# Loading the third batch's q between the W1 chunks of the second batch, and moving beta's split to GpSimd

## Chip, cores, metric

One Trainium2 chip (trn2), one core. The metric is the device time of one execution in microseconds. Executions of one kernel agree within about 0.3%, so differences of 2 us (0.25%) are read here from several rounds against the kernel before on the same chip, and from the traces. Faster or slower is drawn at 2%, or 16 us.

## The reference

Grouped-query attention, then a residual MLP with affine scalings, for 8 batches of 384 rows.

```python
# q [8,16,384,64], k and v [8,4,384,64] float32
scores = matmul(q, k^T) / 8            # k, v repeated 4 times over the heads
x = softmax(scores) @ v                # -> [8, 384, 1024]
a1 = alpha1 * x + beta1
u = x + lam * einsum('ts,bsd->btd', w_tok, a1)
a2 = alpha2 * u + beta2
out = u + lam * (relu(a2 @ w_ch1) @ w_ch2)   # w_ch1 [1024,4096], w_ch2 [4096,1024]
```

## The kernel before

Each batch has two passes on TensorE (PE). In the first, the **W1 pass**, `a2 @ w_ch1` is done in 16 chunks of W1, each 16 matmuls, 2.60 us. W1 does not stay in SBUF: every batch streams it again from HBM, through a ring of five chunk tiles, cast from float32 to bf16 on the way. In the second, the **W2 pass**, PE multiplies by `w_ch2` (which stays in SBUF), and between its matmuls stand the scores, exponentials and token mixing of the next batch. The first batch's attention has no pass to hide in; that is the **lead**.

q and k must stand transposed. From the third batch on, a DMA transpose (a **flip**) does that, from a raw bf16 copy; for the first two batches PE does it.

```python
def load_q(b):                       # four loads of 192 KB, issued by GpSimd
    qrs[b] = sb.tile([P, Hq, NST, D], bf, tag="q_raw", name="q_raw", bufs=1)
    for h in range(0, Hq, G):
        nc.gpsimd.dma_start(out=qrs[b][:, h:h + G], in_=q[b, h:h + G]...)

def flip_queue(b):
    return nc.scalar if b == 2 else nc.sync

# main(b), W1 pass
for c in range(NCH):                 # NCH = 16 chunks, RING = 5
    ...                              # 16 matmuls, evictions on ScalarE and VectorE in turn
    if b or c + RING < NCH:
        load_w1(b * NCH + c + RING)  # into the tile that chunk c has just freed
    if b == 0 and c == NCH - 1:
        for i in range(RING):
            load_w1(NCH + i)
        load_next(2)                 # place k, load q and v of the third batch
# ... the flips of the third batch, placed at steps of the second batch's W1 pass
if b == 1:
    moves = [(0, 46 + 4 * i, flip_q, 2, 2 * i - 2, 2) if i else (0, 46, flip_k, 2) for i in range(5)]

# lead: rows of alpha, beta, lambda are split into bf16 parts on VectorE
def split(lo, hi, step=None):
    ...
    nc.vector.tensor_copy(out=rows_b[:32, c], in_=src[:, c])
    nc.vector.scalar_tensor_tensor(out=dst[:, c], in0=rows_b[:32, c], scalar=m, in1=src[:, c], op0=MUL, op1=subtract)
```

The softmax here doesn't subtract the row's maximum and nothing guards it: scores larger than these inputs give would overflow.

## Time and profile before

| | |
|---|---|
| median (9 runs beside each later set) | 806.1 to 806.6 us |
| span of the profiled run | 803.5 us |
| PE busy | 793.8 us |
| first W1 matmul of the main loop (the lead's end) | 38.48 us |
| first matmul of the second batch's W1 pass | 133.44 us |
| first scores matmul of the third batch | 178.42 us |
| from the one to the other ("the stretch") | 44.98 us |
| the same stretch one batch later | 42.56 us |

"The stretch" holds one W1 pass, four matmuls of the W2 pass and any wait for the third batch's q. Everything else of the second batch cancels out of it. The profile lines are in the prediction. To read the timeline lines: start, length, engine, source line, operation, output<-inputs, shape, count, and in brackets how long the engine was idle before and what ended that.

### The profile page before, as it was taken

How to read it: one execution, taken by the hardware profiler on the slowest of the kernel's cores; microseconds unless marked ns; L12 is line 12 of the kernel's file. 1: busy time of each engine (PE TensorE's matmuls, PEld its weight loads, DVE VectorE, ACT ScalarE, POOL GpSimd, SP SyncE). 2: the span in 40 equal slices, each digit the busy share in tenths (PEclk: the TensorE clock that was granted, in tenths of full speed). 3: DMA queues.
4: the chain of work that ended last, by engine and by line, in shares of the span. 5: the costliest groups of instructions: out<-in, count | busy, mean ns of one | idle time of the engine just before them, and what ended most of it. 6: DMA issues, size and time to landing. Idle time of an engine off the chain costs nothing.

```text
span 803.5 us, 14220 instructions
## 1 busy us (share of the span) xinstructions
PE 793.8 (99%) x6123; PEld 452.0 (56%) x6123; DVE 343.5 (43%) x669; ACT 226.9 (28%) x309; POOL 178.5 (22%) x233
## 2 busy tenths in 40 slices
PE   8999999999999999999999999999999999999997
PEld 4766555655556555565555655566555655556545
DVE  8652465215552266322662236622366225552122
ACT  6624431223402233123221233122431223312100
POOL 7234231332013500135002340033400330003000
PEclk9999999999999999999999999999999999999999
DMA  9999999999269972999439991499914995129611
GB/s 190 202 186 202 205 207 170 187 186 170 66 126 188 198 101 58 162 189 196 74 73 169 193 196 43 92 174 197 163 46 114 165 198 88 48 61 187 82 40 40
DMA packets 234975, 113.17 MB, mean 141 GB/s; under 512 B 84376, under 2 KB 228768, under 8 KB 234912
## 3 DMA queue, kind: packets, MB, share of 16 engines
q0 software_dynamic: 170752, 83.47, 79.1%
q1 hardware_dynamic: 58848, 27.22, 13.5%
q10 hardware_dynamic: 5312, 1.57, 1.5%
q8 instruction: 48, 0.79, 0.4%
q14 instruction: 15, 0.12, 0.0%
HBM read 170.53 MB, written 12.58 MB: 228 GB/s over the span
## 4 chain that ended last, share of the span: by engine, by line
PE 84%; DMA 10%; issue 3%; DVE 1%; POOL 1%; ACT 0%; POOLq 0%
PE ch L443 37%; PE h L410 34%; DMA w<-in_moe_w_ch_dram 8%; PE sc L217 4%; PE sc L252 3%; PE sc L273 3%; DMA qT<-q_raw 1%; POOL w L136 1%; PE h L168 1%; PE tok L273 1%; PE av L252 0%; PE warm L460 0%; PE ut L290 0%; PE tp L203 0%; ACT hT L226 0%
## 5 line engine op out<-in xcount | busy, mean ns | idle before, releaser
L443 PE MATMUL ch<-w,hT 128*128 128x512 bf16 (+2 forms) x1600 | 357.7, 371 | 1.1 <-DVE o L448 0.9
L410 PE MATMUL h<-a2T,w 128*128 128x384 bf16 (+1 forms) x2016 | 331.5, 326 | 0.8 <-ACT hT L418 0.8
L410 PEld LDWEIGHTS <-w 128*128 128x128 bf16 x2016 | 196.8, 98 | 131.2 <-issue 1.5
L443 PEld LDWEIGHTS <-hT 128*128 128x128 bf16 x1600 | 144.6, 98 | 153.1 <-issue 10.5
L136 POOL DMA_DIRECT2D w<-in_moe_w_ch_dram x128 | 112.1, 878 | 519.3 <-PE h L410 500.5
L226 ACT ACTIVATE es<-sc 128x1024 bf16<-128x1024 f32 x126 | 121.4, 1023 | 187.9 <-PE sc L217 175.8
L420 DVE TENSOR_SCALAR hT<-h,bias 128x384 bf16<-128x384 f32 x128 | 79.1, 618 | 218.3 <-PE h L410 217.7
L418 ACT ACTIVATE hT<-h,bias 128x384 bf16<-128x384 f32 x128 | 74.3, 580 | 304.9 <-PE h L410 299.4
L448 DVE TENSOR_TENSOR o<-ch,vecs 128x512 f32<-128x512 f32 (+2 forms) x50 | 33.4, 669 | 107.8 <-PE ch L443 107.8
L252 PEld LDWEIGHTS <-es 128*128 128x128 bf16 x1008 | 38.2, 97 | 13.2
L273 PEld LDWEIGHTS <-wtokT 128*128 128x128 bf16 x576 | 37.3, 98 | 13.8 <-DVE x L258 1.7
L217 PE MATMUL sc<-qT,kT 64*128 64x384 bf16 (+2 forms) x576 | 41.9, 272 | 0.7 <-DMA qT<-q_raw 0.6
L257 DVE RECIPROCAL rinv<-sc 128x6 f32<-128x6 f32 x56 | 10.8, 193 | 68.4 <-PE sc L252 67.5
L252 PE MATMUL sc<-v,es 128*128 128x65 bf16 x1008 | 39.9, 193 | 0.0
L280 DVE TENSOR_TENSOR x<-sc,x 128x384 f32<-128x384 f32 x56 | 31.0, 553 | 20.0 <-PE sc L273 20.0
L273 PE MATMUL sc<-a,wtokT 128*128 128x128 bf16 x504 | 37.3, 219 | 0.0
L217 PEld LDWEIGHTS <-kT 64*128 64x128 bf16 x576 | 21.6, 94 | 24.5 <-issue 18.2
L449 DVE TENSOR_TENSOR o<-o,x 128x512 f32<-128x512 f32 (+2 forms) x50 | 33.5, 670 | 1.7
L284 DVE TENSOR_TENSOR a<-x,vecs 128x384 bf16<-128x384 f32 x56 | 32.7, 584 | 1.9
L265 DVE TENSOR_TENSOR a1f<-x,vecs 128x384 f32<-128x384 f32 x56 | 31.2, 558 | 1.9
L267 DVE TENSOR_TENSOR a<-a1f,vecs 128x384 bf16<-128x384 f32 x56 | 31.2, 558 | 1.9
L258 DVE TENSOR_TENSOR x<-sc,rinv 128x384 f32<-128x384 f32 x56 | 31.2, 558 | 1.9
(75 smaller groups left out, 203.1 us busy)
## 6 DMA issues: line engine op xcount, KB each, us to landing
w<-in_moe_w_ch_dram POOLq DMA_DIRECT2D x144, 512.0 KB, 8.6
out_dram<-o SPq DMA_DIRECT2D x47, 256.0 KB, 2.0
q_raw<-in_q_dram POOLq DMA_DIRECT2D x28, 192.0 KB, 8.1
kst<-in_k_dram SPq DMA_DIRECT2D x16, 192.0 KB, 3.4
v<-in_v_dram POOLq DMA_DIRECT2D x24, 64.0 KB, 7.9
a2T<-a SPq DMA_TRANSPOSE x56, 2.3
qg<-in_q_dram POOLq DMA_DIRECT2D x3, 192.0 KB, 5.9
stage<-in_q_dram ACTq DMA_DIRECT2D x2, 192.0 KB, 3.7
```

The costliest lines, as they stand in the source:

```text
L136: nc.gpsimd.dma_start(out=t, in_=w1src[:, :, c * CW * P:(c + 1) * CW * P])
L217: nc.tensor.matmul(out=sc[:, hh, k % 4:k % 4 + n], lhsT=kT[r, sk, 2 * p // G, :], rhs=qT[r, p, st:st + n, :], start=True, stop=True)
L226: nc.scalar.activation(out=e, in_=sc, func=EXP, scale=scale_qk)
L252: nc.tensor.matmul(out=av[:, hh, sq, :], lhsT=ess[k // 4][:, m % 2, k % 4, :], rhs=vb[:, sk, hk, :], start=(sk == 0), stop=(sk == NST - 1))
L273: nc.tensor.matmul(out=ps[:, tt, :], lhsT=wtokT[:, st, tt * P:(tt + 1) * P], rhs=a1s[p][:, st, :], start=(st == 0), stop=(st == NST - 1 an ...
L284: nc.vector.tensor_tensor(out=a2s[p], in0=u, in1=bc(al2, p), op=MUL)
L410: nc.tensor.matmul(out=ps[:, :n], lhsT=w1[:, dt, j * P:(j + 1) * P], rhs=a2T[:, dt, :n], start=(dt == 0), stop=(dt == NDT - 1))
L418: nc.scalar.activation(out=hT[:, nt, :], in_=ps[:, :S], func=RELU, bias=c1)
L420: nc.vector.tensor_scalar(out=hT[:, nt, :], in0=ps[:, :S], scalar1=c1, scalar2=0.0, op0=ADD, op1=mybir.AluOpType.max)
L443: nc.tensor.matmul(out=ps[:, lo:hi], lhsT=hT[:, nt, ms * P:(ms + 1) * P], rhs=w2[:, nt, dw * 512 + lo:dw * 512 + hi], start=(nt == 0), sto ...
L448: nc.vector.tensor_tensor(out=o[:, lo:hi], in0=ps[:, lo:hi], in1=lam_t[:, c], op=MUL)
L449: nc.vector.tensor_tensor(out=o[:, lo:hi], in0=o[:, lo:hi], in1=x[:, ms, c], op=ADD)
```

## The change

Its intent: take the flips of the third batch off ScalarE's queue, where each holds up evictions for 3 us; load q later, in small parts, out of the way of the W2 loads; and relieve VectorE in the lead.

```diff
-    def load_q(b):
-        qrs[b] = sb.tile([P, Hq, NST, D], bf, tag="q_raw", name="q_raw", bufs=1)
-        for h in range(0, Hq, G):
+    def load_q(b, hs=range(0, Hq, G)):
+        if b not in qrs:
+            qrs[b] = sb.tile([P, Hq, NST, D], bf, tag="q_raw", name="q_raw", bufs=1)
+        for h in hs:
...
-        flip_queue(b).dma_start_transpose(...)      # flip_k and flip_q
+        nc.sync.dma_start_transpose(...)
...
                     load_w1(NCH + i)
-                load_next(2)
+                place_k(2, 0)
+                place_k(2, 1)
+                load_v(2)
+            if b == 1 and c in (3, 5, 7, 9):
+                load_q(2, [(c - 3) * 2])
...
-                moves = [(0, 46 + 4 * i, flip_q, 2, 2 * i - 2, 2) if i else (0, 46, flip_k, 2) for i in range(5)]
+                moves = [(0, 1, flip_k, 2)] + [(0, 46, flip_q, 2, i, 2) for i in range(0, NP, 2)]
... lead: beta's rows on GpSimd, W1 chunks 2 to 4 asked for after them
-        for c in range(RING):
+        load_w1(0)
+        load_w1(1)
+        place_k(0, 1)
+        scale_rows(1, nc.gpsimd)
+        split(1, 2, None, nc.gpsimd)
+        for c in range(2, RING):
             load_w1(c)
-        place_k(0, 1)
... lead: the order of scores, a1, token mixing (18 steps; cut); a part of q asked for before w_tok (cut);
... on GpSimd the split uses two instructions for each scalar_tensor_tensor (cut)
```

More of the change, by code (lines that the diff above doesn't have):

```diff
@@ L41 @@
     ADD = mybir.AluOpType.add
+    SUB = mybir.AluOpType.subtract
     B, Hq, S, D = q.shape
@@ L110, in load_v @@
             nc.gpsimd.dma_start(out=vt[b % 2][:, st, :, :D], in_=by_st(v[b])[:, st])
-    def load_q(b):
-        qrs[b] = sb.tile([P, Hq, NST, D], bf, tag="q_raw", name="q_raw", bufs=1)
-        for h in range(0, Hq, G):
+    def load_q(b, hs=range(0, Hq, G)):
+        if b not in qrs:
+            qrs[b] = sb.tile([P, Hq, NST, D], bf, tag="q_raw", name="q_raw", bufs=1)
+        for h in hs:
             nc.gpsimd.dma_start(out=qrs[b][:, h:h + G], in_=q[b, h:h + G].rearrange("h (p st) d -> p h st d", st=NST))
-    def flip_queue(b):
-        return nc.scalar if b == 2 else nc.sync
     def flip_k(b):
-        flip_queue(b).dma_start_transpose(out=kT.rearrange("p st h s -> p (st h) s"),
+        nc.sync.dma_start_transpose(out=kT.rearrange("p st h s -> p (st h) s"),
                                     in_=k2s[b].rearrange("p st h a d -> p (st h a d)"))
     def flip_q(b, i=0, n=NP):
-        flip_queue(b).dma_start_transpose(out=qT[:, i:i + n].rearrange("p a j s -> p (a j) s"),
+        nc.sync.dma_start_transpose(out=qT[:, i:i + n].rearrange("p a j s -> p (a j) s"),
                                     in_=qrs[b][:, 2 * i:2 * (i + n)].rearrange("p h st d -> p (h st d)"))
@@ L260, in av_piece @@
             if first:
-                a1s[p] = hTf[:, 6144 + p % 3 * S:6144 + (p % 3 + 1) * S].rearrange("p (a d) -> p a d", a=NST)
-                nc.vector.tensor_tensor(out=a1s[p], in0=x[:, :, cols(p)], in1=bc(g1, p), op=MUL)
                 return
@@ L267, in av_piece, with a1 @@
             nc.vector.tensor_tensor(out=a1s[p], in0=t, in1=bc(h1, p), op=ADD)
+        def a1(p):
+            a1s[p] = hTf[:, 6144 + p % 3 * S:6144 + (p % 3 + 1) * S].rearrange("p (a d) -> p a d", a=NST)
+            nc.vector.tensor_tensor(out=a1s[p], in0=x[:, :, cols(p)], in1=bc(g1, p), op=MUL)
         def tok(p):
@@ L375, in side @@
               2: [(q_transpose, 2, 2, "av")], 3: [(warmup, 1), (spread, lower, (0, 1), "tp")],
-              4: [(av, 0)], 5: [(wtok_transpose, 0, "av"), (wtok_transpose, 1, "tp")],
-              6: [(av, 1), (wtok_transpose, 2, "av"), (k_transpose, 2, 2, "tp")], 7: [(q_transpose, 4, 2, "av"), (scale_rows, 1), (split, 1, 2)],
-              8: [(fill_h, 0), (rows_r, "tp"), (av, 2)], 9: [(spread, upper, (0, 1), "av", "ACT"), (q_transpose, 6, 2, "mm")],
-              10: [(tok, 0)],
-              11: [(av, 3)], 12: [(tok, 1), (ut, 0)], 13: [(av, 4), (tok, 2)], 14: [(ut, 1), (fill_h, 4), (tok, 3)],
-              15: [(av, 5), (ut, 2)], 16: [(tok, 4), (ut, 3)], 17: [(av, 6), (tok, 5)]}
+              4: [(av, 0)], 5: [(a1, 0)], 6: [(av, 1), (k_transpose, 2, 2, "tp")],
+              7: [(q_transpose, 4, 2, "av"), (a1, 1)], 8: [(av, 2)],
+              9: [(wtok_transpose, 0, "av"), (wtok_transpose, 1, "tp")],
+              10: [(wtok_transpose, 2, "av"), (q_transpose, 6, 2, "mm"), (fill_h, 0)], 11: [(av, 3), (rows_r, "tp")],
+              12: [(spread, upper, (0, 1), "av"), (a1, 2)], 13: [(tok, 0), (av, 4), (a1, 3)],
+              14: [(tok, 1), (ut, 0), (a1, 4)], 15: [(av, 5), (tok, 2), (a1, 5), (fill_h, 4)], 16: [(ut, 1), (tok, 3)],
+              17: [(ut, 2), (av, 6), (a1, 6)]}
         for i in range(18):
@@ L385, in side @@
                 add(f, *a)
-        for f, *a in ((ut, 4), (h_part, (0, 1), range(4)), (av, 7), (ut, 5), (tok, 6),
-                      (h_part, (2, 3), range(4)), (h_part, range(4), (4,)), (ut, 6), (tok, 7),
+        for f, *a in ((tok, 4), (ut, 3), (h_part, (0, 1), range(3)), (av, 7), (a1, 7), (tok, 5), (ut, 4), (h_part, (0, 1), (3,)),
+                      (tok, 6), (h_part, (2, 3), range(4)), (ut, 5), (tok, 7), (h_part, range(4), (4,)), (ut, 6),
                       (h_part, range(4), (5,)), (ut, 7), (h_part, range(4), (6,)), (h_part, range(4), (7,))):
@@ L515, with scale_rows, split @@
                 nc.vector.tensor_reduce(out=t[:n], in_=ident[:n, :n].rearrange("p (k c) -> p c k", c=NP), op=ADD, axis=AX)
-        def scale_rows(i):
+        def scale_rows(i, eng=nc.vector):
             r = rows_f[:, i * P:(i + 1) * P]
-            nc.vector.tensor_tensor(out=r, in0=r, in1=rows_f[:, 3 * P:4 * P], op=MUL)
-        def split(lo, hi, step=None):
+            eng.tensor_tensor(out=r, in0=r, in1=rows_f[:, 3 * P:4 * P], op=MUL)
+        def split(lo, hi, step=None, eng=nc.vector):
             c = slice(lo * P, hi * P)
@@ L527, in split @@
                     src, dst = (rows_t, rows_f) if i else (rows_f, rows_t)
-                    nc.vector.tensor_copy(out=rows_b[:32, c], in_=src[:, c])
-                    nc.vector.scalar_tensor_tensor(out=dst[:, c], in0=rows_b[:32, c], scalar=m, in1=src[:, c],
-                                                   op0=MUL, op1=mybir.AluOpType.subtract)
+                    eng.tensor_copy(out=rows_b[:32, c], in_=src[:, c])
+                    if eng is nc.vector:
+                        eng.scalar_tensor_tensor(out=dst[:, c], in0=rows_b[:32, c], scalar=m, in1=src[:, c],
+                                                 op0=MUL, op1=SUB)
+                    else:
+                        eng.tensor_scalar(out=dst[:, c], in0=rows_b[:32, c], scalar1=m, scalar2=None, op0=MUL)
+                        eng.tensor_tensor(out=dst[:, c], in0=dst[:, c], in1=src[:, c], op=SUB)
             if step != 0:
-                nc.vector.tensor_copy(out=rows_b[:32, c], in_=rows_f[:, c])
+                eng.tensor_copy(out=rows_b[:32, c], in_=rows_f[:, c])
         def fill_h(p):
@@ L540 @@
         load_v(0)
+        load_q4(2)
         nc.gpsimd.dma_start(out=wtok_in, in_=moe_w_tok.rearrange("(p tt) s -> p tt s", tt=NST))
-        load_q4(2)
         load_q4(3)
         place_k(0, 0, (0,))
-        for c in range(RING):
+        load_w1(0)
[4 more added lines that the diff above has]
+        for c in range(2, RING):
             load_w1(c)
-        place_k(0, 1)
         load_k(1)
```

## Prediction

> **What bounds the kernel now.** I read the page first, then the waits of each engine, then PE's timeline, and the windows where PE was not full. The page says that PE is the bound nearly everywhere, so only its idle time and added waits can move the time.
>
> ```profile
> PE 793.8 (99%) x6123; PEld 452.0 (56%) x6123; DVE 343.5 (43%) x669; ACT 226.9 (28%) x309; POOL 178.5 (22%) x233
> ```
>
> PE is idle for 803.5 - 793.8 = 9.7 us of the span. The change removes no matmul (both programs hold equally many PE rows), so it can win at most that, and part of it is the start and the last store. The windows view, in tens of microseconds, shows that the idle time that lies inside the kernel is in two places (columns: PE, weight load, VectorE, ScalarE, GpSimd busy with counts; granted clock, DMA share, GB/s):
>
> ```profile
> 10.00:20.00 10.00, 7.91 (x125) 5.20 (x121) 9.19 (x27) 7.70 (x10) 5.58 (x9) 1.00 1.44 206
> 20.00:30.00 10.00, 10.00 (x174) 7.89 (x173) 7.70 (x18) 8.86 (x11) 3.92 (x6) 1.00 1.52 194
> ...
> 150.00:160.00 10.00, 10.00 (x64) 6.03 (x62) 2.21 (x4) 2.32 (x4) 3.10 (x5) 1.00 1.43 190
> 160.00:170.00 10.00, 9.81 (x61) 5.79 (x60) 2.12 (x4) 1.78 (x4) 3.40 (x4) 1.00 1.43 195
> 170.00:180.00 10.00, 8.48 (x55) 4.44 (x53) 1.85 (x3) 1.73 (x4) 4.46 (x7) 1.00 1.36 179
> ```
>
> The first place, 10 to 20 us, is the lead, where the first batch's attention runs; there VectorE is 92% busy. The second, 160 to 180 us, is the end of the second batch's first matmul (the "W1 pass": 16 chunks of W1, each 16 matmuls). PE's timeline names what it waited for there:
>
> ```profile
> 18.96 0.34 PE L273 MATMUL tok<-hT,wtokT 128*128 128x128 bf16 x3 [1.43 <-DVE x L258]
> ...
> 133.44 33.96 PE L410 MATMUL h<-a2T,w 128*128 128x384 bf16 x208
> 167.60 2.76 PE L410 MATMUL h<-a2T,w 128*128 128x384 bf16 x16 [0.19 <-ACT hT L418]
> 170.59 2.76 PE L410 MATMUL h<-a2T,w 128*128 128x384 bf16 x16 [0.23 <-ACT hT L418]
> 173.77 2.76 PE L410 MATMUL h<-a2T,w 128*128 128x384 bf16 x16 [0.41 <-ACT hT L418]
> 176.75 1.02 PE L443 MATMUL ch<-w,hT 128*128 128x512 bf16 x4 [0.23 <-ACT hT L418]
> 178.42 0.83 PE L217 MATMUL sc<-qT,kT 64*128 64x384 bf16 x12 [0.64 <-DMA qT<-q_raw]
> ```
>
> ScalarE is late with its evictions because the flips (DMA transposes) of the third batch's k and q are issued from its queue, each holding it for about 3 us:
>
> ```profile
> 166.97 0.58 ACT L418 ACTIVATE hT<-h,bias 128x384 bf16<-128x384 f32 x1 [2.85 <-PE h L410]
> 166.99 2.92 ACTq L125 DMA_TRANSPOSE qT<-q_raw  x1
> 169.96 0.58 ACT L418 ACTIVATE hT<-h,bias 128x384 bf16<-128x384 f32 x1 [2.41 <-PE h L410]
> 170.04 3.05 ACTq L125 DMA_TRANSPOSE qT<-q_raw  x1
> ```
>
> What this costs: from the first matmul of the W1 pass to the first scores matmul takes 178.42 - 133.44 = 44.98 us in the second batch. In the third, where the flips come later and from SyncE, it is 275.06 - 232.50 = 42.56 us. The difference is **2.4 us**.
>
> The second limit is DMA. In the W1 pass a chunk of 512 KB (as bf16) is eaten in 2.60 us, a demand of 524,288 / 2.60 = 202 GB/s. The same windows give 190 to 195 GB/s there, and 195 to 198 in the third batch's pass; with a backlog earlier in the kernel they reach 190 to 210. So the W1 pass runs with the DMA engines full, and lives on a ring of five chunks. A chunk's load is issued when the chunk five before it has been eaten, and must be in 4 chunks later: 4 x 2.60 = 10.4 us, less 0.3 us until the issue starts, so about **10.1 us**. The landing times (issue to landing, minimum, median, maximum), of chunks issued at 155 to 160, 160 to 165, 165 to 170 and 170 to 178 us, one line each:
>
> ```profile
> DMA to landing us min/median/max: 7.4/7.9/7.9
> ...
> DMA to landing us min/median/max: 7.9/8.7/9.4
> ...
> DMA to landing us min/median/max: 11.9/12.8/13.7
> ...
> DMA to landing us min/median/max: 14.9/15.9/16.2
> ```
>
> Undisturbed a chunk lands in 7.9 us: slack 2.1 to 2.2 us. As soon as the flips start (163.8 us) landing goes to 16.2 us, beyond the deadline. It does no harm there, because the chunks issued after 162.5 us belong to the next batch's pass, a second matmul away.
>
> **What the Trainium skill says.** "DMA: Bandwidth & Descriptors", section Issuing engines are not separate DMA queues: DMAs started by ScalarE, SyncE or GpSimd run on the same 16 engines and interleave; another queue saves only the issuing sequencer's time. The trace agrees on both halves: the flips cost ScalarE 3 us each, and they raise W1's landing from 7.9 to 16.2 us although W1 is in another queue. The same page, Specifications, gives a fabric ceiling of 435 GB/s and 358 GB/s of HBM for a core. W1 is float32 in HBM, so 202 GB/s written is 403 GB/s read; that lies between the two, which fits a stream with no room left. "SBUF — State Buffer", section Who interferes with whom: a VectorE instruction with two SBUF inputs contends with a GpSimd one that reads SBUF. It bears on the split moved to GpSimd; in the trace before, GpSimd does too little arithmetic in the lead for me to see it.
>
> **The change part by part.**
> 1. The flips of batch three go from ScalarE's queue to SyncE's. ScalarE's waits go: all of the 2.4 us, as in the third batch, if q arrives in time. **-2.4 us.**
> 2. q is no longer loaded during the first batch's second matmul (issues at 104 to 114 us, landing 17 to 24 us later in a backlog). PE has no wait in that stretch, so relieving it wins 0.
> 3. q is loaded instead after chunks 3, 5, 7 and 9 of the W1 pass, in the same GpSimd queue as W1, and each part is flipped when it lands. This puts new work on full DMA engines, ahead of chunks that have 2.1 us of slack. The last chunk of the pass (15) stands behind all of it but the last flip:
>  - four loads of 192 KB, 786 KB at about 200 GB/s: 3.9 us;
>  - flips: the landing time rose by 16.2 - 7.9 = 8.3 us while k (384 KB) and four q parts (192 KB each) were flipped, so 8.3 x 192 / 1152 = 1.4 us per q part, 2.8 us for k. Three q flips come before chunk 15: 4.1 us;
>  - the flip of k moves to the pass's start, on SyncE ahead of two k loads of the same size that were there (135.5 us) and now follow the flips: 2.8 - 2.0 = 0.8 us.
>  Sum 8.8 us, less 2.1 us of slack: PE waits **6.7 us** in chunks 9 to 15, most of it in the last four. When PE waits, nothing is lost twice: the wait is the DMA work itself.
> 4. The lead. scale_rows and split of beta leave VectorE: six instructions of 0.21 to 0.34 us, 1.7 us; the second spread comes to VectorE from ScalarE, 0.69 us. Net 1.0 us off an engine that is 92% busy. The token-mix weights' transposes move behind scores that ScalarE's exponentials wait for. PE's idle time from 12 to 19 us is 0.22 + 0.44 + 1.43 = 2.1 us, the ceiling. But scores 0 to 10 then hold 9.4 us of PE work (added from the timeline) against eleven exponentials of 0.93 us, 10.2 us, so some 0.8 us of waiting for ScalarE appears instead. GpSimd has time for the split: it comes after two W1 issues, by about 13 us, and the rows need it at about 16 us. **-1.2 us.**
>
> Sum: -2.4 - 1.2 + 6.7 = +3.1 us, 809.5 us from 806.4.
>
> **The rivals.** (a) The transfers are hidden: the DMA engines may take more when more is queued, or the flips finish between packets. For it: 206 to 210 GB/s is seen in some windows, and 202 is needed. Against it: at 163.8 us a full queue did not speed anything up, landing times simply doubled. Then the time is 806.4 - 3.6 = 802.8 us. (b) The wait for W1 takes the place of the waits removed, as summed: 807 to 811 us. (c) The flips are slower than I take them, or the parts land so late that the last flip holds up the first scores as well: one flip more, 1.4 us, and up to 812 us. (d) The lead gets worse through the contention on GpSimd or a transposed order that waits: at most 1 us either way.
>
> **Range and chances.** I give (a) 0.25, (b) and (c) together 0.75, and take 808.8 us, a little below the sum, with 802.5 to 812 us. Two per cent is 16 us, more than all the idle time and more than the whole sum of added DMA work; so within 2% 0.98, faster 0.005, slower 0.015.
>
> **What would show it right or wrong.** In the changed profile: ScalarE's evictions at a steady 2.6 us through the second batch's W1 pass, no wait for ScalarE (step 1). PE waits for W1 there, growing from chunk 9 on, 6.7 us in sum, and landing times over 10.1 us for chunks issued from about 145 us (step 3). The stretch from first W1 matmul to first scores: 49.3 us by my sum, 42.6 by rival (a). PE idle in 10 to 20 us of about 0.9 us (step 4). I would be wrong if landing times in the pass stay below 10 us with q and flips in it, which would mean that the engines were not full; or if the lead moves by over 2 us.

## The result

The changed kernel took 809.62 us (median of 4, 808.24 to 810.36), the kernel before 806.39 us. The ratio is 1.0039, interval 1.0022 to 1.0057. On a second chip it was 809.29 against 806.10 us, ratio 1.0038.

The page of the changed kernel, PE's row of part 1 and the row of the W1 matmuls of part 5 (busy, mean ns | idle just before, releaser):

```profile
PE 793.8 (98%) x6123; PEld 452.1 (56%) x6123; DVE 341.4 (42%) x664; ACT 226.3 (28%) x308; POOL 182.2 (23%) x241
...
L412 PE MATMUL h<-a2T,w 128*128 128x384 bf16 (+1 forms) x2016 | 332.1, 326 | 6.2 <-DMA w<-in_moe_w_ch_dram 6.2
```

PE's work is the same 793.8 us; new is a wait of 6.2 us for W1, which was not there at all. The windows of the changed kernel at both places:

```profile
10.00:20.00 10.00, 9.48 (x164) 6.40 (x161) 8.47 (x23) 9.70 (x12) 9.31 (x16) 1.00 1.40 206
20.00:30.00 10.00, 9.87 (x165) 8.11 (x162) 8.25 (x20) 6.35 (x9) 3.68 (x6) 1.00 1.52 194
...
150.00:160.00 10.00, 9.49 (x59) 5.41 (x57) 2.40 (x4) 2.02 (x4) 5.02 (x6) 1.00 1.45 192
160.00:170.00 10.00, 6.53 (x39) 3.36 (x36) 1.85 (x3) 1.46 (x3) 2.63 (x3) 1.00 1.45 192
170.00:180.00 10.00, 7.74 (x46) 4.33 (x47) 1.24 (x2) 1.74 (x3) 1.75 (x2) 1.00 1.43 191
```

In the lead PE went from 7.91 to 9.48 of 10 us. In the pass it fell to 6.53 of 10 us, while the DMA share stayed at 1.45 and the rate at 191 to 192 GB/s: the DMA engines move no more than before, they only have more to move. PE's timeline there:

```profile
131.52 26.17 PE L412 MATMUL h<-a2T,w 128*128 128x384 bf16 x160
158.21 2.78 PE L412 MATMUL h<-a2T,w 128*128 128x384 bf16 x16 [0.51 <-DMA w<-in_moe_w_ch_dram]
162.50 2.77 PE L412 MATMUL h<-a2T,w 128*128 128x384 bf16 x16 [1.52 <-DMA w<-in_moe_w_ch_dram]
165.97 2.77 PE L412 MATMUL h<-a2T,w 128*128 128x384 bf16 x16 [0.69 <-DMA w<-in_moe_w_ch_dram]
170.18 2.77 PE L412 MATMUL h<-a2T,w 128*128 128x384 bf16 x16 [1.44 <-DMA w<-in_moe_w_ch_dram]
173.51 2.77 PE L412 MATMUL h<-a2T,w 128*128 128x384 bf16 x16 [0.55 <-DMA w<-in_moe_w_ch_dram]
177.80 2.77 PE L412 MATMUL h<-a2T,w 128*128 128x384 bf16 x16 [1.52 <-DMA w<-in_moe_w_ch_dram]
180.41 1.03 PE L449 MATMUL ch<-w,hT 128*128 128x512 bf16 x4
181.37 0.83 PE L216 MATMUL sc<-qT,kT 64*128 64x384 bf16 x12
```

The first ten chunks (160 matmuls) run through; each of the last six waits. The waits for ScalarE and for q are gone. The stretch is 181.37 - 131.52 = 49.85 us, 7.3 us over the third batch's. The sum of the waits shown is 6.2 us. Of the rest, about 1.0 us is the run-out of six chunks: one between waits takes 2.77 or 2.78 us from first start to last end, one in the flow 26.17 / 10 = 2.62 us.

Landing times of W1 chunks in the changed kernel, issued at 133 to 140, 140 to 150, 150 to 155, 155 to 160 and 160 to 165 us:

```profile
DMA to landing us min/median/max: 7.4/8.7/8.8
...
DMA to landing us min/median/max: 8.8/9.3/10.6
...
DMA to landing us min/median/max: 12.3/12.7/13.1
...
DMA to landing us min/median/max: 14.7/15.1/15.5
...
DMA to landing us min/median/max: 16.5/16.5/16.5
```

They pass the 10.1 us of the prediction with the chunk asked for at 147.58 us, which is chunk 10, the first that PE waits for.

The balance of the two profiled runs: the lead ends at 36.56 instead of 38.48 us (-1.92), the stretch is 49.85 instead of 44.98 us (+4.87), together +2.95 us; the spans differ by 806.5 - 803.5 = 3.0 us.

### The profile page after: what moved, and what is told of

It reads as the page before. It is cut to its first block, busy times and chain, and to the rows that moved or that the text cites. A ratio compares the mean times of both kernels' runs of the same rounds, so it can differ in the third digit from the quotient of the medians.

```text
span 806.5 us, 14222 instructions
## 1 busy us (share of the span) xinstructions
PE 793.8 (98%) x6123; PEld 452.1 (56%) x6123; DVE 341.4 (42%) x664; ACT 226.3 (28%) x308; POOL 182.2 (23%) x241
## 4 chain that ended last, share of the span: by engine, by line
PE 94%; DMA 3%; DVE 1%; ACT 1%; issue 0%
PE ch L449 42%; PE h L412 38%; PE sc L216 4%; PE sc L251 4%; PE sc L274 3%; DMA w<-in_moe_w_ch_dram 3%; PE h L167 1%; ACT hT L225 1%; PE tok L274 0%; PE av L251 0%; PE warm L466 0%; PE ut L291 0%; PE tp L202 0%; PE vec L331 0%; PE tok L278 0%
## 5 line engine op out<-in xcount | busy, mean ns | idle before, releaser
L274 PE MATMUL sc<-a,wtokT 128*128 128x128 bf16 x504 | 37.3, 219 | 0.0
```

What stands on the lines that cost most here:

```text
L274: nc.tensor.matmul(out=ps[:, tt, :], lhsT=wtokT[:, st, tt * P:(tt + 1) * P], rhs=a1s[p][:, st, :], start=(st == 0), stop=(st == NST - 1 an ...
```

## The experiments

All were run against the kernel before, on the same chip, in three jobs; medians are those of the fast runs. "Stretch" and "lead's end" are from the profile; "over" is the stretch less 42.56 us.

| run | edit | median us | ratio to before, interval | lead's end | stretch | over |
|---|---|---|---|---|---|---|
| before | | 806.39 | 1 | 38.48 | 44.98 | 2.4 |
| after | the change | 809.62 | 1.0039, 1.0022 to 1.0057 | 36.56 | 49.85 | 7.3 |
| after_again | the change | 809.29 | 1.0038, 1.0023 to 1.0054 | 37.31 | 50.18 | 7.6 |
| lead_only | lead's part alone | 804.91 | 0.9976, 0.9963 to 0.9990 | (no fast profile) | | |
| lead_only_2 | the same | 804.46 | 0.9980, 0.9966 to 0.9994 | 37.31 | 45.26 | 2.7 |
| q_only | q part alone | 811.23 | 1.0057, 1.0044 to 1.0070 | 38.35 | 50.56 | 8.0 |
| no_flips | change, no flips of q | 806.25 | 0.9995, 0.9983 to 1.0008 | 37.30 | 46.68 | 4.1 |
| loads_only_2 | change, no flips of q and k | 804.88 | 0.9983, 0.9969 to 0.9996 | 37.32 | 45.13 | 2.6 |
| early_loads | change, q loaded as before | 808.17 | 1.0026, 1.0010 to 1.0041 | 37.69 | 48.33 | 5.8 |
| ring6 | change, six W1 tiles | 805.35 | 0.9989, 0.9976 to 1.0003 | 37.31 | 46.71 | 4.2 |
| late_sync | q as before, flips late | 807.28 | 1.0014, 1.0000 to 1.0027 | 36.67 | 46.81 | 4.3 |
| split_early | q's parts around the pass | 802.59 | 0.9954, 0.9942 to 0.9967 | 36.70 | 43.18 | 0.6 |
| lead_vec | split_early, split on VectorE | 804.71 | 0.9989, 0.9977 to 1.0002 | 39.63 | 42.98 | 0.4 |

loads_only, the first run of loads_only_2's kernel, had 804.41 us (0.9977, 0.9962 to 0.9993).

### The two halves apart: lead_only, lead_only_2, q_only

lead_only is the changed kernel with load_q, flips and moves as before; q_only is the kernel before with only these changed.

> The kernel before with only the lead's part of the change (beta's split on GpSimd, denser order). If the parts add up: the first W1 matmul of the main loop starts 1.9 us earlier than before (36.6 instead of 38.5 us), the second batch's W1 pass keeps its 45.0 us to the first scores, and the time is 806.4 - 1.9 = 804.5 us. If the lead's gain is lost again where the second batch waits for DMA (the transfers, not PE, set that pace), the time stays at 806.4 us.

> lead_only again, for a profile in the fast state (the first one's profile had matmuls four times as long). First W1 matmul of the main loop at 36.6 us instead of 38.5; the second batch's stretch 45.0 us as before with ScalarE's waits in it; 804.5 to 805.0 us.

> The kernel before with only the q part of the change (parts between the W1 chunks, flips on SyncE). Theory: the stretch from the first W1 matmul of the second batch to its first scores grows from 45.0 to 49.9 us, the time is 806.4 + 4.9 = 811.3 us. Rival (the denser lead pushed DMA work together and the waits for W1 come from that): the stretch stays near 45 us and the time near 806 us.

The lead's part alone gives ratios of 0.9976 and 0.9980 (1.6 to 1.9 us), q's part alone 1.0057 (4.6 us). The excesses add up to 0.33 to 0.37%, and the whole change was 0.38 to 0.39% slower. So the parts hardly interact; the rival for q_only (that the denser lead brought on the waits) falls. lead_only_2's timeline keeps ScalarE's waits and the wait for q:

```profile
172.81 2.76 PE L415 MATMUL h<-a2T,w 128*128 128x384 bf16 x16 [0.41 <-ACT hT L423]
175.82 1.02 PE L448 MATMUL ch<-w,hT 128*128 128x512 bf16 x3 [0.25 <-ACT hT L423]
177.53 0.83 PE L219 MATMUL sc<-qT,kT 64*128 64x384 bf16 x12 [0.69 <-DMA qT<-q_raw]
```

The lead's end came at 36.6 to 36.7 us in some profiled runs of kernels with this lead and at 37.3 to 37.7 us in others, where PE first waits 0.3 to 1.0 us for a spread of alpha. The expectation of 36.6 us was met in part only. What makes this wait come and go was not tested.

### What the loads and the flips cost: no_flips, loads_only, early_loads

no_flips takes away the four flips of the third batch's q, loads_only also k's flip:

```diff
-  moves = [(0, 1, flip_k, 2)] + [(0, 46, flip_q, 2, i, 2) for i in range(0, NP, 2)]
+  moves = [(0, 1, flip_k, 2)]        # no_flips
+  moves = []                         # loads_only
```

> The changed kernel without the four flips of the third batch's q: its result is wrong on purpose. Theory (all transfers share full DMA engines): the three q flips ahead of the last chunk are 4.1 us of the 7.3 us that PE waits, so 3.2 us remain (2.6 by the sum of the prediction); stretch 45.8 us, time 805.5 us. Rival (only what stands in W1's own queue delays W1, flips on another queue do not): 7.3 us remain, stretch 49.9 us, 809.6 us.

> As no_flips, and without the flip of the third batch's k too (result wrong on purpose): only the four q loads are left in the second batch's W1 pass. no_flips lost 4.1 us in the stretch (46.7 against 42.6 us of the third batch). If the sum of the prediction holds, the loads are 3.9 less 2.1 us of slack = 1.8 us: stretch 44.4 us, and the flip of k was the mis-sized term with 2.3 us. If the loads were the mis-sized term, and k costs 0.8 us as predicted, 3.3 us remain: stretch 45.9 us. Time 806.3 less 0.8 to 2.3 us: 804.0 to 805.5 us.

> loads_only again, for a profile in the fast state. In no_flips the k loads of the fourth batch came back to the start of the pass (SyncE is free for them), so it held k's flip and the q loads: 2.8 + 3.9 - 2.1 = 4.6 us by the prediction's terms, 4.1 measured. Here only the q loads remain: 3.9 - 2.1 = 1.8 us, stretch 44.4 us. If it stays at 46 us or more, the loads are the mis-sized term.

Both are wrong: the third batch then uses stale q (and k). By the reference, with these inputs, the largest scaled score of that batch is 0.057, so the softmax is nearly flat; with the second batch's q in the third the whole output would change by 0.5% in norm, the third batch's by 1.5%. A pass in this comparison therefore does not vouch for q. That split_early below loads the right q rests on its code, not on the comparison.

Flips on another queue do delay W1: without them the stretch fell from 49.85 to 46.68 us. The expectation of 45.8 us was missed by 0.9 us, because it overlooked something: SyncE, no longer held up by flips that wait for q, issued the fourth batch's k loads (2 x 192 KB) at 135.92 us again, as in the kernel before, and they cost DMA time at the pass's start. With the terms of the prediction, k's flip and the loads less the slack are 2.8 + 3.9 - 2.1 = 4.6 us; 4.1 us were measured. loads_only_2 then has the four q loads alone in the pass: 2.6 us over, 1.8 expected. The stretch of 45.13 us lies between the two expectations (44.4 and 45.9 us), so both terms were off: the loads were sized too low by 0.8 us, k's flip too high (46.68 - 45.13 = 1.55 us instead of 2.8).

early_loads leaves the loads where they were and lets the flips start from SyncE as soon as q is in:

```diff
-                place_k(2, 0)
-                place_k(2, 1)
-                load_v(2)
-            if b == 1 and c in (3, 5, 7, 9):
-                load_q(2, [(c - 3) * 2])
+                load_next(2)
```

> The changed kernel with q loaded where it was before, its flips on SyncE and free to start as soon as q is in, at the start of the second batch's W1 pass. Theory: the loads' DMA work leaves the pass, that of the flips stays; of 7.3 us some 3.4 us remain, less if the flips still find the DMA engines idle before the first W1 load: stretch 44 to 46 us, time 804 to 806 us. Rival (the split loads are harmless and the flips alone are to blame): the stretch stays near 49.9 us.

It took 808.17 us, over the 804 to 806 us expected, and its stretch of 48.33 us lies nearer to the rival's 49.9 than to the 44 to 46 us; but loads_only_2 showed that the split loads are not harmless. The flips all fell at the start, 134.7 to 146 us, and PE waited there instead:

```profile
132.66 15.97 PE L412 MATMUL h<-a2T,w 128*128 128x384 bf16 x96
150.86 2.77 PE L412 MATMUL h<-a2T,w 128*128 128x384 bf16 x16 [2.23 <-DMA w<-in_moe_w_ch_dram]
155.07 2.77 PE L412 MATMUL h<-a2T,w 128*128 128x384 bf16 x16 [1.44 <-DMA w<-in_moe_w_ch_dram]
158.47 10.68 PE L412 MATMUL h<-a2T,w 128*128 128x384 bf16 x64 [0.62 <-DMA w<-in_moe_w_ch_dram]
169.62 10.57 PE L412 MATMUL h<-a2T,w 128*128 128x384 bf16 x64 [0.47 <-DMA w<-in_moe_w_ch_dram]
```

From 155 us to the pass's end W1 lands in 9.9 to 11 us, at the deadline: the backlog is not worked off in this pass. The expectation had again let the fourth batch's k loads out; here they follow at 146 us. The third batch's pass, which "over" is measured against, has two such loads too (234.5 us), so they cancel: the five flips cost 5.8 + 2.1 = 7.9 us, where the prediction's terms give 8.3 us.

### The ring's depth: ring6

```diff
-    RING = 5
+    RING = 6
-  tag="tmp", name="a1f", bufs=4    # and the same tag's "o"
+  tag="tmp", name="a1f", bufs=2
```

> The changed kernel with a ring of six W1 chunks instead of five; to make room, the temporary tile of the stores and of a1 has two buffers instead of four. Theory (deadline of the ring against full DMA engines): a chunk has 2.6 us longer to land, so 2.6 of the 7.3 us go: stretch 47.3 us, time 807.0 us, and PE's first wait comes about two chunks later. Rival (GpSimd's issue or the order in its queue sets the pace, not the deadline): stretch 49.9 us. If two temporary buffers cost something, it shows as waits of VectorE outside the stretch.

The stretch fell by 3.1 us against the first profile of the change, 3.5 against the second (2.6 expected), and PE ran through 12 chunks (192 matmuls) instead of ten. The timed runs gave 0.50%, 4.0 us (0.9989 against 1.0039), whose intervals leave room for 2.6. The pass's last chunk landed in 16.6 us, as late as with five tiles (16.5 us), and hurt less. So it is the deadline, not the landing time as such, that turns DMA work into a wait. GpSimd's issue as the pace falls: its instructions are the same. The two temporary buffers cost nothing that PE's waits show.

### The flips late: late_sync

q is loaded as before; the flips are held back, because k is copied only after the load of chunk 15:

```diff
+                load_q(2)
                 load_v(2)
-            if b == 1 and c in (3, 5, 7, 9):
-                load_q(2, [(c - 3) * 2])
+            if b == 1 and c == 10:
+                place_k(2, 0)
+                place_k(2, 1)
-  moves = [(0, 1, flip_k, 2)] + ...    # the rest as it was
+  moves = [(0, 46, flip_k, 2)] + ...
```

> The changed kernel with q loaded where it was before (first batch's second matmul), and the flips on SyncE held back by placing k only after the load of the last W1 chunk of the second batch's pass. Theory: neither ScalarE's waits nor W1's late landings are left; the stretch is 42.6 us as in the third batch, the time 809.6 - 7.3 = 802.3 us, faster than both. Rival (the flips cost the same DMA time wherever they are in the pass): the last chunk still lands late, or the first scores wait for q; the stretch is 45 us or more and the time 804.5 us or more.

This missed: 807.28 us instead of 802.3. W1 was nearly in time (one wait of 0.17 us), but the scores were not:

```profile
171.00 2.77 PE L412 MATMUL h<-a2T,w 128*128 128x384 bf16 x16 [0.17 <-DMA w<-in_moe_w_ch_dram]
173.61 1.03 PE L449 MATMUL ch<-w,hT 128*128 128x512 bf16 x3
178.48 0.83 PE L216 MATMUL sc<-qT,kT 64*128 64x384 bf16 x12 [3.84 <-DMA qT<-q_raw]
```

The first flip of q was issued at 166.4 us and landed 12.1 us later, against 2.8 us in a W2 pass of the kernel before without W1 loads beside it. The theory had counted a flip by its share of DMA work (1.4 us) and forgotten its latency. The Trainium skill, "DMA: Bandwidth & Descriptors", section Queues, rings and completion order, says that a DMA engine takes the queues that have work for it in turn, packet by packet. The trace agrees in number: from 166.4 to 178.5 us, 2,644 packets of the flips' queue and 2,553 of W1's were moved, about one for one; before 166.4 us none of the flips' were. (Whether the profile's packets are those of the page is not shown.) An estimate from that: k's flip and the first part of q are 1,536 + 768 packets of 256 B; with as many W1 packets of 512 B between them this is 1.77 MB, which takes 11.0 us at the 161 GB/s of these 12.1 us. No run tests this turn-taking by itself.

The wait cost more than its 3.84 us. After it the granted clock was 0.50 from 180 to 182 us and 0.71 to 184 us, and the next 16 W2 matmuls took 5.31 us, where split_early's took 3.63 us: 1.7 us more, outside the stretch. All five runs have mean clocks of 0.995 to 0.998, so this is part of the missed 5.0 us. That the wait brought the clock down is not shown; after early_loads' longest wait, 2.23 us, the clock stayed at 1.00.

### Around the pass: split_early

The first part of q is loaded early and flipped with k at the start of the pass; the others are loaded only after the last chunk of the pass has been asked for. Their scores come later in the W2 pass.

```diff
+                load_q(2, [0])
                 load_v(2)
-            if b == 1 and c in (3, 5, 7, 9):
-                load_q(2, [(c - 3) * 2])
+            if b == 1 and c in (10, 11, 12):
+                load_q(2, [(c - 9) * 4])
-  moves = [(0, 1, flip_k, 2)] + [(0, 46, flip_q, 2, i, 2) for i in range(0, NP, 2)]
+  moves = [(0, 1, flip_k, 2), (0, 2, flip_q, 2, 0, 2)] + [(0, 58, flip_q, 2, i, 2) for i in range(2, NP, 2)]
```

> The changed kernel with k and the first part of q loaded in the first batch's second matmul and flipped at the start of the W1 pass, and the other three parts of q loaded only after the last W1 chunk of the pass has been asked for (after chunks 10, 11, 12) and flipped as they land. late_sync showed that a flip takes 12 us to land among W1 loads, and that the first scores then wait 3.8 us for the first part. Theory: only k's flip and one q flip (1 us) fall on W1's deadlines, at the pass's start where they have most slack, and the scores of the other parts come 10 us and more into the second matmul. Stretch 42.6 to 43.6 us, time 802.3 to 803.3 us, faster than before by 0.4%. Rival: the later parts' loads and flips are late for their scores, or hold back the next pass's W1: waits of the scores for q, and over 804 us.

802.59 us, ratio 0.9954: faster than the kernel before by 0.46%, and by 0.85% than the change (0.9954 over 1.0039, each against before, on different chips). The stretch is 43.18 us. PE's waits of this kernel:

```profile
PE warm L467 <- DVE wtokT L470: 1.5, 1, 1.5
PE ch L450 <- issue: 1.1, 7, 0.2
PE ch L450 <- DVE o L455: 0.9, 2, 0.5
PE sc L216 <- ACT hT L225: 0.5, 1, 0.5
PE h L412 <- DMA w<-in_moe_w_ch_dram: 0.3, 1, 0.3
PE sc L216 <- ACT qT L204: 0.2, 1, 0.2
```

W1 costs 0.3 us, and no scores wait for a flip, although the chunks for the next batch land in up to 20 us: nobody needs them yet. The same loads and flips, most of them moved to where nothing has a deadline, cost next to nothing. As in the change, the fourth batch's k loads come only after the pass (183 us); what that alone gives here was not tested apart.

### What helped in the lead: lead_vec

split_early, with scale_rows and split of beta back on VectorE, at the step where the kernel before has them.

> split_early with beta's scaling and split back on VectorE (at the step where before had them), in the denser order: tells which half of the lead's part gave the 1.9 us. If the denser order gave it, 802.6 us as split_early and the first W1 matmul of the main loop at 36.6 us; if the 1.7 us taken off VectorE gave it, up to 804.3 us and the first W1 matmul at up to 38.3 us, with PE waiting for VectorE between 10 and 20 us.

804.71 us, ratio 0.9989 against 0.9954 of split_early: 0.35%, or 2.8 us, for six small instructions. PE's timeline in the lead, two lines of it:

```profile
11.36 0.40 PE L216 MATMUL sc<-qT,kT 64*128 64x384 bf16 x4 [0.47 <-ACT hT L225]
17.43 0.33 PE L303 MATMUL tp<-ident,stage 128*128 128x128 bf16 x3 [1.85 <-DVE wtokT L306]
```

The split stands on VectorE ahead of the eviction that PE's transposes wait for, and PE waits 1.85 us; in split_early the same transposes start at 15.62 us, 1.81 us earlier. On GpSimd the split took longer, from 9.76 to 14.04 us in the changed kernel, but nothing waits for it before 16.6 us.

The rest of the 2.8 us is something else. After that wait the granted clock fell (it stands before the DMA share):

```profile
19.00:21.00 2.00, 2.00 (x13) 0.76 (x11) 0.94 (x3) 1.02 (x2) 0.74 (x1) 0.51 1.45 197
21.00:23.00 2.00, 2.00 (x25) 1.40 (x25) 1.81 (x5) 1.84 (x2) 0.74 (x1) 0.64 1.45 198
```

In split_early it was 1.00 there. The lead ends 39.63 - 36.70 = 2.93 us later than in split_early; 1.81 us are the wait, and the other 1.1 us come with the low clock. The timed runs have it too: the mean clock is 0.996 to 0.998 in all five, 1.000 in all of split_early's. Whether the wait brings the clock down was not tested; the kernel before waits 1.43 us in its lead at a clock of 1.00.

The denser order alone gives about nothing, by estimate: the lead's end less the clock's 1.1 us is 38.5 us, as in the kernel before (38.48). In time, 806.1 - 2.0 = 804.1 us would be due with the old lead (the stretch explains 44.98 - 42.98 = 2.0 us), and 804.7 - 1.1 = 803.6 us are left.

### The change again: after_again

> The changed kernel once more, on the chip of the following runs, since its runs lay between 808.2 and 810.4 us: 809.6 us, ratio to before 1.004. Its profile may fall in the state that the first kernel of the two earlier jobs showed (matmuls two to four times as long).

It came out as expected, and shows the spread between executions: the stretch was 50.18 us here and 49.85 us in the first profile.

## Why the prediction was right

**The bound** was read rightly: PE's busy time did not change (793.8 us), and its waits in two places are the whole difference.

**Step 1, ScalarE's waits (-2.4 us), held.** They are gone, and kernels in which neither W1 nor q is late have stretches of 42.98 and 43.18 us, close to the 42.56 us it was measured against.

**Step 2, relieving the first batch's W2 pass wins 0, held.** From the lead's end to the second batch's first W1 matmul it takes 133.44 - 38.48 = 94.96 us before and 131.52 - 36.56 = 94.96 us after.

**Step 3, the new wait for W1 (+6.7 us), held in mechanism and nearly in size.** Full DMA engines, a deadline of 10.1 us and 2.1 us of slack gave 6.7; the two profiles show 7.3 and 7.6. The terms, worked out from the runs and adding slack where it was used: q loads 2.6 + 2.1 = 4.7 us (3.9 predicted); k's flip 1.55 us (2.8); a q flip (5.8 + 2.1 - 1.55) / 4 = 1.6 us (1.4); from these, what the displaced k loads gave back is 4.7 + 1.55 + 3 x 1.6 - 2.1 - 7.3 = 1.7 us (2.0). These are four terms from four runs, on the assumption that the pieces add; no run is left over to test it. "Chunks 9 to 15" was one chunk early, and "most of it in the last four" was 4.2 of the 6.2 us of waits. Rival (c), first scores held up by the last flip, did not come.

**Step 4, the lead (-1.2 us), held, and was if anything sized too low.** The timed runs give 1.6 to 1.9 us, with intervals that reach from 0.5 to 3.0 us; the lead's end came 1.92 us earlier in the first profile of the change and 1.17 us in the second. VectorE's relief was counted as a share of a busy engine; lead_vec shows that it matters by its place, just before an eviction on PE's path (1.8 us). That the denser order adds about nothing of its own is an estimate. The wait for ScalarE's exponentials that was to appear (0.8 us) is 0.47 us, and PE is idle for 0.52 us from 10 to 20 us (0.9 predicted). Of rival (d), contention with GpSimd, VectorE shows nothing: its a1 product took 0.56 us before and 0.54 to 0.56 us after.

**The sum** (809.5 us) met the measured 809.6 us closer than its terms did: step 3 was 0.6 to 0.9 us low and step 4 by up to 0.7 us, with opposite signs; that is luck. The predicted 808.8 us lay below the sum because of 0.25 for rival (a), hidden transfers. That rival fell: landing times went to 16.5 us at 192 GB/s, against 190 to 195 GB/s before.

## What to carry over

A stream that already fills the DMA engines has no gaps to load other things into: here, what was put between its chunks was paid in full, once the ring's slack was spent, by the engine that consumes it. Put such loads where the stream's next chunks have no deadline, and check both sides: what the new transfer delays, and how late the new transfer itself lands (a flip that is 1.6 us of DMA work took 12 us from issue to landing). A ring one tile deeper moved the deadline by one chunk time (2.6 us) and took 3.1 to 3.5 us off the stretch; 4.2 us of the loss stayed. And look at the granted clock after a long wait of PE: in two kernels here a low clock followed one and cost 1.1 and 1.7 us more.

## What the Trainium skill lacked or had wrong

- "DMA: Bandwidth & Descriptors" (Specifications, Bandwidth) gives ceilings of 358 and 435 GB/s without saying which side counts for a load that casts. Here float32 loads into bf16 stood at 190 to 198 GB/s written in the W1 passes of the second and third batch. By the sizes that is 380 to 396 GB/s read, above the 358 on this one core, and it did not rise with more queued (191 to 192 GB/s at landing times of 16.5 us).
- The same page gives a bandwidth for DMA transposes but no landing time beside other loads: a q part took 2.8 us without W1 loads, 8.2 us (after) and 12.1 us (late_sync) among them.
- "TensorE: Matmul & The Clock Gate" (Part 1) knows warm and cold clocks and warns that recorded clock events can be unreliable, with a quarter rate seen for over 50 us. Two profiled executions here (lead_only, loads_only) were slow throughout, each the first program of its job: 2936 and 1674 us, with the granted clock shown as 1.00. Their matmuls of 512 columns took 1100 and 675 ns on average, 380 ns in the kernel before. Neither was explained, and neither is used for a time.
